# A gated mix of a spectral filter and a state-space scan on one core: A's inner steps sent through DRAM, first and last stage in 64x64 matmul tiles

## The chip, the cores and the metric

The kernel runs on one core of a Trainium2 chip, in fp32 throughout. The metric is the device time of one execution in microseconds (us), given as the median of several runs. A core has TensorE (PE, with weight loads shown apart as PEld), VectorE (DVE), ScalarE (ACT), GpSimd (POOL) and SyncE (SP), which here issues most DMA transfers; DMAs are also issued by POOL. PE reads from SBUF and writes PSUM, whose pool `ps` has four buffers of 128 partitions x 2 x 512 fp32 in this kernel.

## The reference

x has 2048 positions (L) and 512 channels (D). Two linear operators act on it, and a gate mixes them:

```python
x = A_x
g = _sigmoid((x * gate_w).sum(-1, keepdims=True))
a = irfft2(rfft2(x) * (w_r + 1j * w_i))             # share A, over positions and channels
K = 2 * Re(sum_n C[d, n] * exp(A[d, n] * dt[d] * l))
b = causal_convolution(x, K) + x * D_skip           # share B, for each channel
return g * a + (1 - g) * b
```

## The kernel before, in words

For share B the kernel assumes that every channel's kernel K is level over the sequence, so that the convolution is a running sum with one coefficient a channel; it counts the channels for which the data allow that (`count`) and enters a general path after the main one (`tc.If`) only where the count is below D. With these inputs it isn't entered.

Share A is a two-dimensional real transform written as matmuls. The 2048 positions are split into 32 x 64 and the 512 channels into folded quarters. The steps are these:

- Ten parts of x (`PARTS`) come by DMA. `fold` (L228, L229, on DVE or POOL) adds and subtracts the halves of a part into a buffer `f`; `C_` (L236, PE) multiplies by `s1e`, into PSUM; `c_a` (L240, DVE) writes a transpose in 32x32 blocks to `AR`.
- Nine units u follow, each for one slot pair `pr` of the inner frequencies: `P_` (L351) and `t_a` (L356), `D_` (L365) and `d_a` (L372), `Z_` (L378, L379) on DVE, `z_a` and `z_b` for one row, the filter weights `W_`, `U` (L400 to L405) on DVE, `p_a` and `g_a` (L412 to L425) on POOL, `h_a`, then the way back: `I_` (L440), `i_a` (L445), `V_` (L453, into `AI`), `B_` (L478 to L481) and `e_a` (L485, ACT, back into `AI`). The letters v, w, j, K, E, H do parts of the last three steps for unit 8.
- When all units are in `AI`, `b_a` (L503) transposes it in place on DVE, eight times 128x1024. `Q_` (L528) multiplies its rows by the constants `s1a`, four matmuls for each of eight output groups j.

Share B: `load_x` fetches x turned (XT, 1 MB for each of four shares), `x_a` (L277, ACT) multiplies it by the coefficient, `scan` (L283, DVE) takes the running sum v. The skip term is then joined in one of two ways: `skip` (L286, ACT) and `both` (L289), an accumulating DMA issued by POOL that adds v to XT; or `skip2` (L292, DVE). `Y_` (L511, PE) turns XT back to rows of positions by `T.transpose`, eight for each j, and `s_a` (L516, ACT) multiplies by 1 - g into `AR`, which by then is free. The gate itself is `G_` (L300 to L308).

The two meet at the output. For most j, `q_a` (L549, DVE) takes Q's PSUM times g plus `AR`; for one j, `a_a` (L539, ACT) takes it out of PSUM and `A_a` (L543, POOL) adds it. `store` (L532) issues two 256-KB stores for each j from SP.

The order of all of this is written out by hand, in the string `PLAN`: each word is a letter for a function and a number for its argument, and each engine gets its instructions in that order. So does SP with its DMAs: one that waits holds back all behind it. `R` words are loads of constants, `l` of filter weights, `X` of XT, `S` of `s1a`.

Of the kernel before, what the change touches and what calls it, by code (L numbers as in the profile page):

```python
# [26 lines left out]
ALU = mybir.AluOpType  # L27
# [25 lines left out]
PARTS = [slice(a, b) for a, b in zip([0, 8, 16, 32, 48, 64, 80, 96, 112, 120], [8, 16, 32, 48, 64, 80, 96, 112, 120, 128])]  # L53
CHANNELS = np.concatenate([_T, 256 + _T, 511 - _T, 255 - _T])


def _consts():
# [14 lines left out]
    s1e = np.zeros((2, 32, 2, 2, 2, 2, 16))  # L72
    for dh in range(2):
        for h in range(2):
            for g in range(2):
                s1e[dh, :, g, g, :, h] = S1[:, :, :16] * (-1) ** (dh * h)
# [35 lines left out]
    s2p = s2p.transpose(1, 0, 2)  # L112
# [41 lines left out]
def body(ctx: ExitStack, tc: tile.TileContext, x, xg, xt, w, wh, prms, vecs, gw, dskip,  # L154
# [48 lines left out]
    with tc.manual_schedule():  # L203
# [19 lines left out]
        def fold(q, E):  # L223
            k = PARTS[q]
            n = 32 * (k.stop - k.start)
            f = t_["f", q] = blk([P, 2, 512], "f")
            xv = X[:, 64 * k.start:64 * k.stop].rearrange("p (u n) -> p u n", u=2)
            E.tensor_tensor(f[:, 0, :n], xv[:, 0], xv[:, 1], op=ALU.add)  # L228
            E.tensor_tensor(f[:, 1, :n], xv[:, 0], xv[:, 1], op=ALU.subtract)  # L229


        def C_(q):
            n = 32 * (PARTS[q].stop - PARTS[q].start)
            p = t_["c", q] = psum("p_s1")
            for u in range(2):
                T.matmul(p[:, u, :n], s1e, t_["f", q][:, u, :n], start=True, stop=True)  # L236
# [58 lines left out]
        def G_(k):  # L295
# [160 lines left out]
        def M_(u):  # L456
            p = t_["pi", u] = psum("p_v").rearrange("p u (h n) -> p u h n", h=2)
            for v in range(nrow(UNITS[u]) // 64):
                for h in range(2):
                    a = [t_["gt", u][:, o, v, 2 * h:2 * h + 2].rearrange("p c k -> p (c k)") for o in range(2)]  # L460
                    T.matmul(p[:, v, h], a[0], dbw[:, h, 0:1].broadcast_to([P, 2, P]), start=True, stop=False)
                    T.matmul(p[:, v, h], a[1], dbw[:, h, 1:3], start=False, stop=True)

        def o_a(u, ks=slice(0, 2)):
            pr = UNITS[u]
            n = nrow(pr) // 64
            ai = AI[:, 2 * pr:2 * pr + n].rearrange("p s (h k t) -> p s h k t", h=2, k=2)
            pi = t_["pi", u][:, :n].rearrange("p s h (k t) -> p s h k t", k=2)
            S.copy(ai[:, :, :, ks], pi[:, :, :, ks])


        def B_(u):
            pr = UNITS[u]
            p = t_["pb", u] = psum("p_ia")
            for v in range(2):
                sl = 2 * pr + v
                if sl == 0:
                    T.matmul(p[:, v], s2e[:, 0], AI[:, 0], start=True, stop=False)  # L478
                    T.matmul(p[:, v], s2e[:, 16], AI[:, 16], start=False, stop=True)
                else:  # L480
                    T.matmul(p[:, v], s2p, AI[:, sl], start=True, stop=True)  # L481

        def e_a(u):
            pr = UNITS[u]
            S.copy(AI[:, 2 * pr:2 * pr + 2], t_["pb", u])  # L485


        def half(u, k):
            pr = UNITS[u]
            return AI[:, 2 * pr:2 * pr + 2].rearrange("p s (h k t) -> p k s h t", h=2, k=2)[:, k]  # L490

        def B2_(u, k):
            if k == 0:
                t_["pb", u] = psum("p_ia").rearrange("p k (s h t) -> p k s h t", s=2, h=2)
            for v in range(2):
                T.matmul(t_["pb", u][:, k, v], s2p, half(u, k)[:, v], start=True, stop=True)

        def e2_a(u, k):
            S.copy(half(u, k), t_["pb", u][:, k])

        def b_a(c):
            v = VA[:, :, 32 * c:32 * c + 32].rearrange("p b d -> p d b")
            V.transpose(v, v)  # L503


        def Y_(j):
            p = t_["py", j] = psum("p_y").rearrange("p k (b i d) -> p (k b) i d", b=2, i=2)
            xv = XT.rearrange("p (i e) (c b) -> p i (e c) b", i=2, b=32)
            for k in range(4):
                for i in range(2):  # L510
                    T.transpose(p[:, k, i], xv[:, i, :, 4 * j + k], eye)  # L511

        def s_a(j):
            for k in range(4):
                b = 4 * j + k
                S.activation(AR[:, b].rearrange("p (i d) -> p i d", i=2), t_["py", j][:, k], AF.Copy, scale=g1[:, 1, b:b + 1])  # L516
# [4 lines left out]
        def load_a(k):  # L521
            s1a[k] = work.tile([P, 8, P], F32, tag="w", name="s1a", bufs=4)
            nc.sync.dma_start(s1a[k], c_s1a[:, 8 * k:8 * k + 8])

        def Q_(j):
            p = t_["pq", j] = psum("p_oa").rearrange("p k (b d) -> p (k b) d", b=2)
            for k in range(4):
                T.matmul(p[:, k], s1a[j // 2][:, 4 * j % 8 + k], VA[:, 4 * j + k], start=True, stop=True)  # L528
# [17 lines left out]
        def q_a(j):  # L546
            for k in range(4):
                b = 4 * j + k
                V.scalar_tensor_tensor(AR[:, b], t_["pq", j][:, k], g1[:, 0, b:b + 1], AR[:, b], op0=ALU.mult, op1=ALU.add)  # L549
# [28 lines left out]
    with tc.If(n_small < D):  # L578
        with tc.tile_pool(name="dram", bufs=1, space=bass.MemoryType.DRAM) as dp:
# [137 lines left out]
            for e in range(2):  # L717
                nc.sync.dma_start(dsg[64 * e:64 * e + 64], dskip[256 * e:256 * e + 256].rearrange("(o d) -> o d", o=1).broadcast_to([64, 256]))
# [76 lines left out]
```

## Time and profile before

| what | value |
|---|---|
| runs shown | 148.42, 150.05, 151.9 us; median 150.05 |
| profiled execution | 148.65 us, of which the span is 146.8 |
| busy in the span | PE 112.6, DVE 113.8, ACT 70.5, POOL 57.4 us |
| DMA | 25.52 MB, mean 174 GB/s |
| mean granted TensorE clock | 0.95 |

Times inside the program count from the span's start. In a group's row the first number is the busy time of all its instructions together, the second the mean length of one in ns; overlapping instructions are counted once in the first. Behind the second bar stand the idle time of the engine just ahead of them, and what ended it. An fp32 matmul appears as two records, a transpose as one.

### The profile page before, as it was taken

The numbers are of one execution on the slowest core, as the hardware profiler recorded it, in microseconds if no ns is written. First come the engines' busy times: TensorE is split into PE (matmuls) and PEld (weight loads), VectorE is DVE, ScalarE is ACT, GpSimd is POOL, SyncE is SP. The second block draws the span as 40 slices with busy tenths as digits, with TensorE's granted clock in tenths as the row PEclk, the third lists the DMA queues.
The fourth block names the chain that finished last, engine by engine and source line by source line (L and its number), as shares of the span: only waits on it lengthen the run. The fifth ranks groups of instructions, "written<-read, shape, count | busy, mean of one in ns | idle before, by whom it ended". The sixth has DMA issues, their size and how long they took to land.

```text
span 146.8 us, 1834 instructions
## 1 busy us (share of the span) xinstructions
PE 112.6 (77%) x611; PEld 86.1 (59%) x611; DVE 113.8 (78%) x134; ACT 70.5 (48%) x136; POOL 57.4 (39%) x57
## 2 busy tenths in 40 slices
PE   7936976399989998959888878997805975999600
PEld 7811352098978982858378577462405964888400
DVE  0369999995788597759798995979689997695900
ACT  0003000337375969496789765398610699504000
POOL 0306850100059993976999979200200000003300
PEclk9999999959999999999999999999975899999985
DMA  4999999992105870404793898000191000158690
GB/s 114 318 275 418 391 417 387 413 416 99 37 7 173 287 292 0 143 5 146 132 225 91 273 214 210 4 0 0 40 214 36 0 0 0 57 205 318 223 354 19
DMA packets 9427, 25.52 MB, mean 174 GB/s; under 512 B 1568, under 2 KB 2624, under 8 KB 8512
## 3 DMA queue, kind: packets, MB, share of 16 engines
q1 hardware_dynamic: 8976, 22.16, 42.2%
q0 software_dynamic: 432, 3.15, 10.9%
q8 instruction: 7, 0.11, 0.3%
q14 instruction: 12, 0.10, 0.2%
HBM read 17.93 MB, written 4.19 MB: 151 GB/s over the span
## 4 chain that ended last, share of the span: by engine, by line
DVE 31%; PE 30%; ACT 17%; DMA 9%; issue 5%; POOL 2%; SPq 1%; DVEq 0%; ACTq 0%; POOLq 0%
DVE AR L240 9%; PE p_oa L528 8%; PE p_d L365 6%; ACT AR L516 6%; PE p_t L351 5%; DMA XT<-v 5%; PE p_v L440 5%; DMA AI<-in_x_dram 5%; DVE v L283 3%; DVE p_d L378 3%; DVE p_d L379 3%; DVE tw L405 3%; PE p_ia L481 2%; PE p_y L511 2%; DVE AR L549 2%
## 5 line engine op out<-in xcount | busy, mean ns | idle before, releaser
L351 PEld LDWEIGHTS p_t<-s2e,AR 128*128 128x128 f32 x136 | 17.4, 208 | 5.5 <-DVE AR L240 3.5
L351 PE MATMUL p_t<-s2e,AR 128*128 128x128 f32 x136 | 18.0, 294 | 3.4 <-DVE AR L240 2.7
L440 PEld LDWEIGHTS p_v<-dbw,gt 128*128 128x128 f32 x136 | 16.0, 192 | 7.5 <-issue 4.6
L440 PE MATMUL p_v<-dbw,gt 128*128 128x128 f32 x136 | 16.8, 278 | 4.6 <-ACT gs L303 1.5
L236 PE MATMUL p_s<-f,AI 128*128 128x512 f32 (+1 forms) x40 | 15.7, 527 | 5.5 <-DVE f L228 3.4
L412 POOL TENSOR_TENSOR px<-tw 128x512 f32<-128x512 f32 (+1 forms) x9 | 10.9, 1215 | 19.6 <-DVE tw L405 19.5
L503 DVE STREAM_TRANSPOSE AI<-AI 128x1024 f32<-128x1024 f32 x8 | 16.9, 2202 | 1.8 <-ACT AI L485 1.8
L365 PE MATMUL p_d<-et,dfw 128*128 128x256 f32 (+1 forms) x72 | 16.1, 371 | 0.7 <-ACT et L356 0.6
L240 DVE STREAM_TRANSPOSE AR<-p_s 128x1024 f32<-128x1024 f32 (+1 forms) x10 | 14.8, 1555 | 1.6 <-PE p_s L236 1.6
L516 ACT ACTIVATE AR<-p_y,g 128x256 f32<-128x256 f32 x32 | 11.8, 587 | 8.1 <-PE p_y L511 8.1
L528 PE MATMUL p_oa<-AI,s1a 128*128 128x256 f32 x64 | 14.1, 380 | 1.7 <-ACT AR L516 1.7
L511 PE MATMUL p_y<-eye,XT 128*128 128x128 f32 x64 | 10.0, 317 | 6.5 <-DMA XT<-v 5.6
L277 ACT ACTIVATE p_x<-XT,pers 128x1024 f32<-128x1024 f32 x8 | 9.0, 1121 | 12.5 <-POOL pers L261 10.4
L549 DVE SCALAR_TENSOR_TENSOR AR<-p_oa,g,AR 128x256 f32<-128x256 f32 x28 | 11.6, 477 | 4.2 <-PE p_oa L528 4.0
L236 PEld LDWEIGHTS p_s<-f,AI 128*128 128x128 f32 x40 | 7.1, 196 | 13.1 <-issue 4.3
L365 PEld LDWEIGHTS p_d<-et,dfw 128*128 128x128 f32 x72 | 12.7, 190 | 2.5 <-ACT et L356 1.2
L528 PEld LDWEIGHTS p_oa<-AI,s1a 128*128 128x128 f32 x64 | 12.1, 190 | 3.5 <-ACT AR L516 1.9
L543 POOL TENSOR_TENSOR AR<-AR,qs 128x1024 f32<-128x1024 f32 x1 | 2.3, 2348 | 29.2 <-ACT qs L539 29.2
L511 PEld LDWEIGHTS p_y<-eye,XT 128*128 128x128 f32 x64 | 9.2, 201 | 7.8 <-issue 6.3
L453 DVE TENSOR_TENSOR AI<-p_v,po 128x512 f32<-128x512 f32 (+1 forms) x18 | 10.9, 650 | 2.3 <-ACT po L445 2.3
L405 DVE TENSOR_TENSOR tw<-p_d,w 128x1024 f32<-128x1024 f32 x8 | 9.8, 1219 | 3.6 <-ACT p_d L390 3.6
L481 PE MATMUL p_ia<-AI,s2p 128*128 128x512 f32 x26 | 12.0, 595 | 0.0
(66 smaller groups left out, 180.6 us busy)
## 6 DMA issues: line engine op xcount, KB each, us to landing
w<-in_w_dram SPq DMA_DIRECT2D x8, 512.0 KB, 5.6
XT<-in_xt_dram SPq DMA_DIRECT2D x4, 1024.0 KB, 7.0
out_dram<-AR SPq DMA_DIRECT2D x16, 256.0 KB, 3.7
AI<-in_x_dram SPq DMA_DIRECT2D x6, 512.0 KB, 7.6
XT<-v POOLq DMA_DIRECT2D x3, 1024.0 KB, 7.0
s1a<-in_c_s1a_dram SPq DMA_DIRECT2D x4, 512.0 KB, 3.9
AI<-in_x_dram SPq DMA_DIRECT2D x4, 256.0 KB
prm<-in_prms_dram SPq DMA_DIRECT2D x3, 256.0 KB
```

Source lines behind the costliest of these rows:

```text
L236: T.matmul(p[:, u, :n], s1e, t_["f", q][:, u, :n], start=True, stop=True)
L240: V.transpose(AR.rearrange("p s (u d) -> p u d s", u=2)[:, :, PARTS[q]], t_["c", q][:, :, :32 * n].rearrange("p u (b d) -> p u d b", d=n))
L351: T.matmul(p[:, q, :, 64 * v:64 * v + 64], AR[:, 16 * (q // 2) + sl, 128 * (q % 2):128 * (q % 2) + 128], s2e[:, k], start=True, stop=True)
L365: T.matmul(p[:, o, :, h, :n], dfw[:, 2 * h + o], et[:, ::-1] if h else et, start=True, stop=True)
L405: E.tensor_tensor(t.rearrange("p o r a k -> p (o r a k)"), z.rearrange("p o q k -> p (o q k)"), w.rearrange("p o r a k -> p (o r a k)"), o ...
L440: T.matmul(p[:, v, h, o], t_["gt", u][:, o, v, 2 * h:2 * h + 2].rearrange("p c k -> p (c k)"), dbw[:, h, o], start=True, stop=True)
L481: T.matmul(p[:, v], s2p, AI[:, sl], start=True, stop=True)
L503: V.transpose(v, v)
L511: T.transpose(p[:, k, i], xv[:, i, :, 4 * j + k], eye)
L516: S.activation(AR[:, b].rearrange("p (i d) -> p i d", i=2), t_["py", j][:, k], AF.Copy, scale=g1[:, 1, b:b + 1])
L528: T.matmul(p[:, k], s1a[j // 2][:, 4 * j % 8 + k], VA[:, 4 * j + k], start=True, stop=True)
L549: V.scalar_tensor_tensor(AR[:, b], t_["pq", j][:, k], g1[:, 0, b:b + 1], AR[:, b], op0=ALU.mult, op1=ALU.add)
```

## The change

**First stage.** The folds are gone. The host lays out x so that the two halves of a position pair lie in partitions 0 to 63 and 64 to 127, in swapped order for every other part. `C_(q)` now does parts q and q + 1 together: 16 matmuls with 64 rows of contraction and 64 output partitions (`tile_position` (r, o)), the sum over u taken in PSUM. The ten loads of x are issued one behind another; `ldt` and `prm` come behind them (R10, R11).

**Inner steps.** `V_` writes `ai` and `e_a` writes `ei`, both blocks of the work pool, in place of `AI`. `b_a(u)` stores `ei` to a DRAM tile `ad` in two DMAs, in 1-KB runs, and `b_b(p)` reads the slot pairs p and p + 4 back in one 1-MB DMA, 32 partitions of `VA` by 32 KB. The eight transposes of L503 and the half steps of unit 8 are removed.

**Last stage.** `Y_` does 16 ordinary matmuls against `eye` for each j, each into 64 output partitions, in place of eight transposes. `Q_` does eight matmuls in 64x64 tiles in place of four in 128x128. Rows are taken in the order `LAST`; `s1a` is half as large and comes in two loads of 512 KB in place of four. Three j (1, 5, 7) take the way over ACT and POOL, five over DVE; the new `PLAN` ends with `Y7 Y1 s7 s1 Y5 s5 b1 w2 Y2 s2 w0 Y6 s6 Y0 Q2 q2 s0 Q1 a1 Q0 q0 Q5 Q6 q6 Q7 a5 G4 a7 A1 Y4 s4 A5 Q4 G5 q4 Y3 A7 s3 Q3 q3`, where w is `b_b`. The gate's DMA is cut in four. `count` moves from stage 1 to the end.

```diff
+LAST = np.array([2 * j + k % 2 + 16 * (k // 2) for j in range(8) for k in range(4)])
...
-        def fold(q, E):
...
-            f = t_["f", q] = blk([P, 2, 512], "f")
-            xv = X[:, 64 * k.start:64 * k.stop].rearrange("p (u n) -> p u n", u=2)
-            E.tensor_tensor(f[:, 0, :n], xv[:, 0], xv[:, 1], op=ALU.add)
-            E.tensor_tensor(f[:, 1, :n], xv[:, 0], xv[:, 1], op=ALU.subtract)
...
         def C_(q):
             n = 32 * (PARTS[q].stop - PARTS[q].start)
-            p = t_["c", q] = psum("p_s1")
-            for u in range(2):
-                T.matmul(p[:, u, :n], s1e, t_["f", q][:, u, :n], start=True, stop=True)
+            p = [psum("p_s1"), psum("p_s1")]
+            t_["c", q], t_["c", q + 1] = p
+            xv = [X[:, 64 * k.start:64 * k.stop].rearrange("p (u n) -> p u n", u=2) for k in PARTS[q:q + 2]]
+            for f in range(2):
+                for u in range(2):
+                    for h in range(2):
+                        for r in (0, 64):
+                            o = r ^ 64 * h
+                            T.matmul(p[h][o:o + 64, f, :n], s1e[r:r + 64, f * u], xv[h][r:r + 64, u], start=u == 0, stop=u == 1, tile_position=(r, o))
...
-        def b_a(c):
-            v = VA[:, :, 32 * c:32 * c + 32].rearrange("p b d -> p d b")
-            V.transpose(v, v)
+        def b_a(u):
+            k, p = divmod(UNITS[u], 4)
+            if ("ad", p) not in t_:
+                t_["ad", p] = dr.tile([2, 4, 2, 2, 32, 256], F32, name=f"ad{p}")
+            for g in range(2):
+                nc.sync.dma_start(t_["ad", p][g, :, k].rearrange("v c b d -> (c b) v d"), t_["ei", u][g::2].rearrange("p s (e d) -> p (s e) d", e=2))
+
+        def b_b(p):
+            nc.sync.dma_start(VA[p::4].rearrange("p b d -> p (b d)"), t_["ad", p].rearrange("g v k c b d -> (g v k c) (b d)"))
...
-            xv = XT.rearrange("p (i e) (c b) -> p i (e c) b", i=2, b=32)
+            xv = XT.rearrange("p (i e) (a g b) -> p i g b (e a)", i=2, g=2, b=32)
             for k in range(4):
                 for i in range(2):
-                    T.transpose(p[:, k, i], xv[:, i, :, 4 * j + k], eye)
+                    for g in range(2):
+                        T.matmul(p[64 * g:64 * g + 64, k, i], xv[:, i, g, LAST[4 * j + k]], eye, start=True, stop=True, tile_position=(0, 64 * g))
...
-            for k in range(4):
-                T.matmul(p[:, k], s1a[j // 2][:, 4 * j % 8 + k], VA[:, 4 * j + k], start=True, stop=True)
+            for k in (0, 2, 1, 3):
+                for r in (0, 64):
+                    o = r ^ 64 * (k // 2)
+                    T.matmul(p[o:o + 64, k], s1a[j // 4][r:r + 64, 4 * (j % 4) + k], VA[r:r + 64, LAST[4 * j + k]], start=True, stop=True, tile_position=(r, o))
```

`PLAN` is new as a whole, so the order of each engine is shown where it matters. On DVE at the start of the program, before the change (p_s1 is C_'s PSUM, f a folded part, prm the parameters of B):

```order
L228 TENSOR_TENSOR f_113<-AI_64 128x256
L229 TENSOR_TENSOR f_113<-AI_64 128x256
L240 STREAM_TRANSPOSE AR_68<-p_s1_116 128x2x8x32
L228 TENSOR_TENSOR f_124<-AI_64 128x512
L229 TENSOR_TENSOR f_124<-AI_64 128x512
L228 TENSOR_TENSOR f_129<-AI_64 128x512
L229 TENSOR_TENSOR f_129<-AI_64 128x512
L240 STREAM_TRANSPOSE AR_68<-p_s1_120 128x2x8x32
L240 STREAM_TRANSPOSE AR_68<-p_s1_138 128x2x16x32
```

And after it, at the same place:

```order
L237 STREAM_TRANSPOSE AR_70<-p_s1_110 128x2x8x32
L237 STREAM_TRANSPOSE AR_70<-p_s1_111 128x2x8x32
L237 STREAM_TRANSPOSE AR_70<-p_s1_132 128x2x16x32
L237 STREAM_TRANSPOSE AR_70<-p_s1_133 128x2x16x32
L237 STREAM_TRANSPOSE AR_70<-p_s1_152 128x2x16x32
L237 STREAM_TRANSPOSE AR_70<-p_s1_153 128x2x16x32
L243 TENSOR_REDUCE last_72<-prm_82 128x4
L244 TENSOR_REDUCE last_72<-prm_83 128x4
L237 STREAM_TRANSPOSE AR_70<-p_s1_179 128x2x16x32
L237 STREAM_TRANSPOSE AR_70<-p_s1_178 128x2x16x32
```

DVE now waits for PE's pairs in the order of the parts, with nothing between them.

On DVE at the end, before the change (v the running sums, p_oa the PSUM of Q):

```order
L292 SCALAR_TENSOR_TENSOR XT_69<-XT_69,pers_70,v_723 128x1024
L453 TENSOR_TENSOR AI_64<-p_v_739,po_748 128x4x128
L283 SCALAR_TENSOR_TENSOR v_723<-pers_70,v_723,p_x_754 128x1024
L453 TENSOR_TENSOR AI_64<-p_v_739,po_748 128x4x128
L283 SCALAR_TENSOR_TENSOR v_671<-pers_70,v_671,p_x_762 128x1024
L292 SCALAR_TENSOR_TENSOR XT_69<-XT_69,pers_70,v_723 128x1024
L503 STREAM_TRANSPOSE AI_64<-AI_64 128x32x32 x8
L549 SCALAR_TENSOR_TENSOR AR_68<-p_oa_892,g1_62,AR_68 128x256 x4
```

And after it:

```order
L280 SCALAR_TENSOR_TENSOR v_800<-pers_73,p_x_775 128x1024
L280 SCALAR_TENSOR_TENSOR v_800<-pers_73,v_800,p_x_802 128x1024
L454 TENSOR_TENSOR ai_827<-p_v_819,po_824 128x2x128 x2
L289 SCALAR_TENSOR_TENSOR XT_71<-XT_71,pers_73,v_800 128x1024 x2
L529 SCALAR_TENSOR_TENSOR AR_70<-p_oa_969,g1_62,AR_70 128x256 x4
```

Two skip2 end DVE's work before the outputs, where one skip2 and the eight transposes stood.

On SP, behind the loads of weights, after the change (ei the unit's result, ad its DRAM tile); before it, the last loads of `s1a` and then the stores of the output stood there:

```order
L477 DMA ad3_696<-ei_688 64x4x256 x2
L477 DMA ad3_696<-ei_701 64x4x256 x2
L480 DMA VA_64<-ad3_696 32x8192
L477 DMA ad2_814<-ei_798 64x4x256 x2
L477 DMA ad2_814<-ei_809 64x4x256 x2
L477 DMA ad0_839<-ei_817 64x4x256 x2
L477 DMA ad0_839<-ei_837 64x4x256 x2
L480 DMA VA_64<-ad2_814 32x8192
L480 DMA VA_64<-ad0_839 32x8192
```

The read of a pair of units stands behind its four stores; the last two reads come one behind another.

More of the change, by code (lines that the diff above doesn't have):

```diff
@@ L70, in _consts @@
         S1[:, 1, s] = -np.sin(2 * pi * a * f / 32)
-    s1e = np.zeros((2, 32, 2, 2, 2, 2, 16))
+    s1e = np.zeros((2, 2, 32, 2, 2, 2, 16))
     for dh in range(2):
         for h in range(2):
-            for g in range(2):
-                s1e[dh, :, g, g, :, h] = S1[:, :, :16] * (-1) ** (dh * h)
+            for k in range(2):
+                s1e[:, dh, :, k, :, h] = S1[:, :, :16] * (-1) ** (dh * h + k)
     s1f = np.zeros((2, 2, 32, 2, 2, 2, 32))
@@ L167, in body @@
     count = keep.tile([1, 1], I32, name="count")
-    AI = keep.tile([P, 17, D], F32, name="AI")
-    VA = AI[:, 0:16].rearrange("p s (e d) -> p (s e) d", e=2)
+    VA = keep.tile([P, 32, 256], F32, name="VA")
+    dr = ctx.enter_context(tc.tile_pool(name="dr", bufs=1, space=bass.MemoryType.DRAM))
     wst = ExitStack()
@@ L178, in body @@
     XT = work.tile([P, 4, L], F32, name="XT")
-    X = AI.rearrange("p s d -> p (s d)")[:, 0:8192]
-    last = AI[:, 16]
-    s1e, ones = last[:, 0:128], last[:, 128:256]
+    X = VA.rearrange("p s d -> p (s d)")
+    last = work.tile([P, 388], F32, name="last")
+    s1e, ones = last[:, 0:128].rearrange("p (k m) -> p k m", k=2), last[:, 128:256]
     hw = last[:, 256:328].rearrange("p (q r f m) -> p q r f m", q=9, r=2, f=2)
@@ L304, in G_ @@
             elif k == 2:
-                for e in range(2):
-                    nc.sync.dma_start(g1[64 * e:64 * e + 64, 0], t_["gs"][0:P:32])
+                gv = t_["gs"].rearrange("p (a g b) -> p g a b", g=2, b=32)
+                for g in range(2):
+                    for e in range(2):
+                        nc.sync.dma_start(g1[64 * g + 32 * e:64 * g + 32 * e + 32, 0], gv[0:P:32, g])
             elif k == 3:
@@ L450, in V_ @@
             n = nrow(pr) // 64
-            ai = AI[:, 2 * pr:2 * pr + n].rearrange("p s (h k t) -> p s h k t", h=2, k=2)
+            if 0 in ks:
+                t_["ai", pr] = blk([P, 2, D], "ai")
+            ai = t_["ai", pr][:, :n].rearrange("p s (h k t) -> p s h k t", h=2, k=2)
             for k in ks:
                 V.tensor_tensor(ai[:, :, :, k], t_["pi", u][:, :n, :, 0], t_["po", u][:, :n], op=ALU.subtract if k else ALU.add)
[L456 to L469, printed above, removed]
         def B_(u):
@@ L475, in B_ @@
             for v in range(2):
[L476 to L479, printed above, removed]
+                if 2 * pr + v == 0:
+                    T.matmul(p[:, v], s2e[:, 0], t_["ai", 0][:, 0], start=True, stop=False)
+                    T.matmul(p[:, v], s2e[:, 16], t_["ai", 8][:, 0], start=False, stop=True)
                 else:
-                    T.matmul(p[:, v], s2p, AI[:, sl], start=True, stop=True)
+                    T.matmul(p[:, v], s2p, t_["ai", pr][:, v], start=True, stop=True)
@@ L483, in e_a @@
         def e_a(u):
[L484 to L496, printed above, removed]
@@ L513, in s_a @@
         def s_a(j):
             for k in range(4):
-                b = 4 * j + k
-                S.activation(AR[:, b].rearrange("p (i d) -> p i d", i=2), t_["py", j][:, k], AF.Copy, scale=g1[:, 1, b:b + 1])
+                b = LAST[4 * j + k]
+                S.activation(AR[:, 4 * j + k].rearrange("p (i d) -> p i d", i=2), t_["py", j][:, k], AF.Copy, scale=g1[:, 1, b:b + 1])
         s1a = {}
         def load_a(k):
-            s1a[k] = work.tile([P, 8, P], F32, tag="w", name="s1a", bufs=4)
@@ L523, in load_a @@
-            nc.sync.dma_start(s1a[k], c_s1a[:, 8 * k:8 * k + 8])
+            s1a[k] = work.tile([P, 16, 64], F32, tag="w", name="s1a", bufs=4)
+            nc.sync.dma_start(s1a[k], c_s1a[:, 16 * k:16 * k + 16])
         def Q_(j):
             p = t_["pq", j] = psum("p_oa").rearrange("p k (b d) -> p (k b) d", b=2)
-            for k in range(4):
-                T.matmul(p[:, k], s1a[j // 2][:, 4 * j % 8 + k], VA[:, 4 * j + k], start=True, stop=True)
+            for k in (0, 2, 1, 3):
+                for r in (0, 64):
+                    o = r ^ 64 * (k // 2)
+                    T.matmul(p[o:o + 64, k], s1a[j // 4][r:r + 64, 4 * (j % 4) + k], VA[r:r + 64, LAST[4 * j + k]], start=True, stop=True, tile_position=(r, o))
```

96 lines of the change are left out of this document (52 added, 44 removed).

## The prediction

> **What bounds the kernel now.** I read the page first, for the span, the engines and the shares of the chain that ended last.
>
> ```profile
> span 146.8 us, 1834 instructions
> PE 112.6 (77%) x611; PEld 86.1 (59%) x611; DVE 113.8 (78%) x134; ACT 70.5 (48%) x136; POOL 57.4 (39%) x57
> DVE 31%; PE 30%; ACT 17%; DMA 9%; issue 5%; POOL 2%; SPq 1%; DVEq 0%; ACTq 0%; POOLq 0%
> ```
>
> DVE and PE are both busy for three quarters of the span and share the chain, so no engine alone sets the end, and the stages must be read one by one. The next view is the last chain in order of time; these are its pieces at the borders of stages (start, length, what).
>
> ```profile
> 104.58 6.97 DMA XT<-v
> ...
> 111.68 3.45 PE p_y L511 x15
> 115.15 8.87 ACT AR L516 x24
> ...
> 124.06 12.34 PE p_oa L528 x56
> ...
> 139.34 0.47 DVE AR L549
> ```
>
> It ends with a transfer (v added into XT by GpSimd's queue), then Y's transposes on PE, their scaling on ACT, then Q on PE. The last store goes out at 139.8. I cut the span at these points, with the first P at 29.6; the columns are the stretch, busy time of PE, weight loads, DVE, ACT and POOL with instruction counts, the granted clock, the DMA share and GB/s.
>
> ```profile
> 0.00:29.60 29.60, 20.40 (x68) 11.60 (x68) 22.59 (x30) 2.61 (x3) 9.64 (x17) 1.00 0.94 342
> 29.60:105.20 75.60, 67.49 (x414) 53.23 (x415) 62.72 (x70) 53.50 (x96) 45.20 (x39) 0.98 0.45 133
> 105.20:124.00 18.80, 10.62 (x66) 9.16 (x64) 16.92 (x9) 9.86 (x26) 0.25 (x1) 0.82 0.28 56
> 124.00:139.80 15.80, 14.05 (x64) 12.08 (x64) 11.60 (x28) 4.50 (x13) 2.35 (x1) 1.00 0.54 195
> 139.80:146.80 7.00, 0.00 (x0) 0.00 (x0) 0.01 (x1) 0.00 (x0) 0.00 (x0) 0.68 0.48 177
> ```
>
> Stage 1 (x in, first transform) is filled by DVE; the middle (units u) by PE and DVE together; the third stretch by DVE's in-place transposes, beside the late transfer and Y; the fourth by PE's Q. The last 7.0 us are the stores landing and the end of the program, which I keep as they are, since the last output row still leaves by the same 256-KB stores. The profiled execution took 148.65 us, 1.85 over its span; the median of the runs shown is 150.05, 1.4 more. I sum against the profile and add the 1.4 at the end.
>
> **Stage 1.** The change drops the folds and makes C_ a set of 16 quarter-size matmuls for each pair of parts. By the groups of instructions (count, busy us, mean ns, idle before):
>
> ```profile
> L228 DVE TENSOR_TENSOR f<-AI 128x512 f32<-128x512 f32 (+1 forms) x6 | 3.5, 590 | 4.6 <-DMA AI<-in_x_dram 4.6
> L229 DVE TENSOR_TENSOR f<-AI 128x512 f32<-128x512 f32 (+1 forms) x6 | 3.5, 588 | 0.0
> L240 DVE STREAM_TRANSPOSE AR<-p_s 128x1024 f32<-128x1024 f32 x6 | 11.3, 1901 | 0.0
> L240 DVE STREAM_TRANSPOSE AR<-p_s 128x512 f32<-128x512 f32 x4 | 4.1, 1035 | 1.6 <-PE p_s L236 1.6
> L259 DVE TENSOR_REDUCE pers<-prm 128x4 f32<-128x512 f32 x1 | 0.7, 675 | 0.0
> 5.04 0.72 POOL L228 TENSOR_TENSOR f<-AI 128x256 f32<-128x256 f32 x1 [4.59 <-DMA AI<-in_x_dram]
> 9.00 0.69 DVE L228 TENSOR_TENSOR f<-AI 128x512 f32<-128x512 f32 x1 [1.23 <-DMA AI<-in_x_dram]
> 11.60 1.27 POOL L228 TENSOR_TENSOR f<-AI 128x512 f32<-128x512 f32 x1 [5.16 <-DMA AI<-in_x_dram]
> 30.00:32.00 2.00, 2.00 (x11) 2.00 (x11) 1.96 (x1) 0.92 (x1) 0.00 (x0) 0.50 1.05 432
> L300 PE MATMUL p_gate<-XT,gws 128*32 128x512 f32 x32 | 3.6, 595 | 0.0
> L481 PE MATMUL p_ia<-AI,s2p 128*128 128x512 f32 x26 | 12.0, 595 | 0.0
> ```
>
> DVE loses 3.5 + 3.5 = 7.0 us of folds. What stays is 15.4 us of transposes, three reduces (2.0) and 0.4 of small work. What do four quarter tiles cost on PE? The trace has no 64x64 tile. The nearest row is the gate: 16 matmuls of 512 columns in four column tiles took 3.64 us, while the 13 full matmuls of 512 columns of L481 took 12.0, 0.92 each. Four column tiles therefore ran in the time of one. I take the same for four 64x64 tiles: a pair of 512-column parts takes 16/4 x 0.91 = 3.6 us, a 256-column pair 1.8. The other end is that only two of the four run at once, 7.3 and 3.6; that is rival one. Below 3.6 the bound is that all 16 took less than four full matmuls, for which no row speaks.
>
> Now the walk. The waits above show parts 0 and 1 landed by 5.0, part 2 at 9.0 and part 4 by 11.6; I take part 3 at 9.7. Since a pair needs both parts, C0 runs 5.5 to 7.3, c0 and c1 end at 9.4. C2 runs 9.7 to 13.3; c2 and c3 follow, 15.2 and 17.1. C4 runs 13.3 to 16.9, c4, c5 end at 20.9, the two reduces at 22.2. C6 must wait for the PSUM buffers of c2 and c3: 17.1 to 20.7, well before DVE wants it; c7 and c6 end at 26.0, the reduce and J0 at 27.1. By the order, half of C8 waits for the buffer of c6, so it ends at 27.8 and c8, c9 at 29.9. **T, the end of stage 1, is 29.9 against 29.6**: the 7.0 us of folds go, and waits for pairs (2.4 at the start, 0.3 and 3.9 before C2's result, 0.7 at the end) take their place. With x landing about 1 us earlier, because the three prm loads no longer stand among its parts, T is near 28; with a PE clock halved after the idle gap before C8, as the granted clock of 0.50 in 30 to 32 shows it after PE's idle time there, it is near 32.
>
> **The middle.** Its DVE rows are the same scans, Z, W, U and V_ instructions: 62.7 us busy of 75.6. The half steps of unit 8 become whole ones (nothing on balance), and 16 stores and four reads join SP's queue in place of nothing, beside DMA rings that were 45% busy. Walking the new order with the old durations, I get 76 us from T to the last skip2 (k6), so **S, the start of Y, is 29.9 + 76 = 105.9**. The part that is new is what Y waits for. Before it waited for the transfer:
>
> ```profile
> POOL XT L289 <- ACT XT L286: 13.2, 2, 11.8
> PE p_y L511 <- DMA XT<-v: 5.6, 1, 5.6
> XT<-v POOLq DMA_DIRECT2D x3, 1024.0 KB, 7.0
> ```
>
> GpSimd sat idle for 11.8 us before it could issue the last one, as the scan and skip that feed it came last; now the last share is finished by skip2 on DVE instead and r0, the last transfer, is issued about 65 us after T. With the 7.0 of its row it lands at T + 73, 3 us ahead of k6. So Y starts at 105.9 and not 111.7: **5.8 us gained**. Should r0 go out 4 us later than I walk it, 1 us of that comes back.
>
> **The last stage.** These rows price it.
>
> ```profile
> L503 DVE STREAM_TRANSPOSE AI<-AI 128x1024 f32<-128x1024 f32 x8 | 16.9, 2202 | 1.8 <-ACT AI L485 1.8
> L511 PE MATMUL p_y<-eye,XT 128*128 128x128 f32 x64 | 10.0, 317 | 6.5 <-DMA XT<-v 5.6
> L516 ACT ACTIVATE AR<-p_y,g 128x256 f32<-128x256 f32 x32 | 11.8, 587 | 8.1 <-PE p_y L511 8.1
> L528 PE MATMUL p_oa<-AI,s1a 128*128 128x256 f32 x64 | 14.1, 380 | 1.7 <-ACT AR L516 1.7
> L549 DVE SCALAR_TENSOR_TENSOR AR<-p_oa,g,AR 128x256 f32<-128x256 f32 x28 | 11.6, 477 | 4.2 <-PE p_oa L528 4.0
> L539 ACT ACTIVATE qs<-p_oa,g 128x256 f32<-128x256 f32 x4 | 1.6, 474 | 6.0 <-PE p_oa L528 6.0
> L543 POOL TENSOR_TENSOR AR<-AR,qs 128x1024 f32<-128x1024 f32 x1 | 2.3, 2348 | 29.2 <-ACT qs L539 29.2
> 36.24 3.73 PE L351 MATMUL p_t<-s2e,AR 128*128 128x128 f32 x32
> XT<-in_xt_dram SPq DMA_DIRECT2D x4, 1024.0 KB, 7.0
> out_dram<-AR SPq DMA_DIRECT2D x16, 256.0 KB, 3.7
> s1a<-in_c_s1a_dram SPq DMA_DIRECT2D x4, 512.0 KB, 3.9
> ```
>
> The 16.9 us of L503 disappear from DVE. In their place the last unit goes through DRAM: two 256-KB stores of ei, then the read of 1 MB. The trace has neither; the nearest rows are the 256-KB output store, 3.7 us, and the 1-MB read of XT, 7.0. The store is issued about 0.5 after S, so the last read lands at S + 0.5 + 3.7 + 7.0, about **S + 11.3**. From below, a 512-KB s1a read took 3.9 on calmer rings, which puts it near S + 8; from above, 32 partitions instead of 128 and 1-KB runs could double both, S + 22.
>
> The Trainium skill bears on this read: "DMA: Bandwidth & Descriptors", in its part on the anatomy of one DMA, gives a fixed 2 us plus bytes over 436 GB/s. By that the store would be an estimated 2.6 us and the read 4.4, and the round trip would be over before PE is through with Y. The XT row's 7.0 for the same 1 MB, under load, speaks against using it, and the sum above does not.
>
> PE is not idle meanwhile. Y now has 16 ordinary matmuls a j in column pairs. 16 such matmuls of 128 columns took 3.73 us (the p_t stretch, 32 records); two at once, as in the gate, make 1.87 a j, against 10.0/8 = 1.25 for the transposes. Six Y before the first Q are 11.2 us: Q2 starts at **S + 11.5**, with the read just landed. Q has eight matmuls of 256 columns a j, four at once: 2 x 0.46 = 0.9, against 14.1/8 = 1.76. ACT's s takes 4 x 0.37 = 1.5, a 1.6, DVE's q 4 x 0.41 = 1.7, POOL's A 2.35 and is hidden twice, since the last two outputs are DVE's. After Q2, Q1, Q0, Q5, Q6, Q7 (5.4) come Y4 (1.9), Q4 (0.9), Y3 (1.9), s3 (1.5) and q3 (1.7): the last q ends at S + 11.5 + 13.3 = S + 24.8. ACT, the next in line, has s0, three a and two s after S + 11.2, 9.3 us, and is no later.
>
> **Sum.** 29.9 + 76 + 24.8 + 7.0 = 137.7 us span, against 146.8: 5.8 from Y's earlier start, 3.3 from Q and the missing transposes. With 1.85 that is 139.6 for an execution like the profiled one, and with the 1.4 to the median **141 us**.
>
> **Rival one: the quarter tiles run two at a time** (slower). A 512 pair then takes 7.3 us, more than the 3.8 in which DVE empties it. C2 ends at 17.0, C4 at 24.3, C6 at 31.6, C8 at 35.2, and T is 39; S is 115. Q takes 1.8 a j, seven on the path, 6.3 more: the end is S + 31, the span 153, the median's scale 156. It decides from a pair of 5.5 us on: there T is about 33.5 and each Q 0.4 longer, and the gain of 9 has shrunk to about 2. For it speaks that nothing in the trace has two row tiles write one PSUM bank; against it the gate, where the column tiles did run together. The Trainium skill, "TensorEngine Tiling (Array Packing)", Gotcha 1, says that different row tiles cannot access the same PSUM bank simultaneously. Here r = 0 and r = 64 write the two partition halves of one bank in each pair, so by that rule the 64x64 tiles would run in twos and the sum would be that of this rival; no row here has row tiles to test it. Chance 0.12.
>
> **Rival two: the trip through DRAM is late.** Should the two legs take 1.6 times their rows, Q2 waits to S + 17.5, PE is idle for 6 us, and Y4 and Y3 stand behind the waiting Q2: 6 us more, 147 on the median's scale, no change. For it: runs of 1 KB and a 32-partition target, and a w2 read on the rings just ahead; against it: rings that were 28% busy there. Chance 0.18.
>
> **Rival three: it goes better.** x lands earlier, T is 27.5 to 28, the read is over early and Y runs faster than p_t did; the last stage is then 22: 135 to 136. Chance 0.12. That the change does nothing is no case, as whole groups go.
>
> **How the numbers follow.** The forecast has 0.58, with 138 to 144 as its own range (T 1.9 lower to 2.1 higher, r0 1 late). 2% is about what a measurement of this kernel can tell from no change, that is 147 and 153. Faster: 0.58 + 0.12 + half of rival two, 0.79. Slower: rival one without its milder forms, 0.10; the rest, 0.11, within 2%. The range leaves out rival one, 0.12, and the late tail of rival two: 134 to 149.
>
> **What would show it.** A pair of C_ at 3.6 us (rival one: 7); the first P at 30; Y's first matmul about 106 with skip2 and not XT<-v ahead of it; Q2 waiting under 1 us for the VA read; the last q at S + 25. Wrong would make it above all a C_ pair over 5 us, a VA read over 10, or DVE in the middle waiting for PE more than before.

## The result, and the profile after

The changed kernel takes **138.68 us** (median; 137.66 to 142.19), the kernel before, on the same chip, 150.63. The ratio is 0.927, with a 95% interval of 0.907 to 0.947: faster by 7%. The ratios, here and below, leave out executions more than 1.5% above the fastest of their kernel, so they are not quotients of the medians. The forecast was 141 in a range of 134 to 149. The profiled execution took 137.66 us, 135.9 of it the span.

The page of the changed kernel, first its span, the engines and the chain:

```profile
span 135.9 us, 2591 instructions
PE 114.1 (84%) x983; PEld 86.1 (63%) x983; DVE 87.7 (65%) x106; ACT 74.4 (55%) x143; POOL 53.8 (40%) x51
PE 44%; DVE 20%; DMA 13%; ACT 11%; issue 4%; SPq 2%; POOL 0%; DVEq 0%; ACTq 0%; POOLq 0%
```

DVE lost 26 us of work (113.8 to 87.7), PE gained 1.5, and the chain moved from DVE to PE. The span cut at the same events as before: the first P, Y's start, Q's start, the end of the last q.

```profile
0.00:27.30 27.30, 22.30 (x181) 11.82 (x182) 16.77 (x19) 3.00 (x5) 1.20 (x9) 0.94 0.91 335
27.30:102.90 75.60, 68.84 (x410) 53.93 (x411) 62.62 (x67) 54.20 (x95) 45.49 (x39) 0.96 0.70 206
102.90:115.30 12.40, 11.18 (x192) 11.01 (x193) 0.00 (x0) 9.01 (x24) 0.00 (x0) 1.00 0.87 311
115.30:128.90 13.60, 11.77 (x200) 9.30 (x200) 8.34 (x21) 8.23 (x22) 7.09 (x3) 1.00 0.68 247
128.90:135.90 7.00, 0.00 (x0) 0.00 (x0) 0.00 (x0) 0.00 (x0) 0.00 (x0) 0.55 0.38 138
```

Stage 1 is 2.3 us shorter. From the first P to Y's start it is 75.6 us, where before Y started 82.1 after P. From Y's start to the last q it is 26.0, before 28.1. The stores at the end take the same 7.0. Stage 1 by its timeline, PE and DVE (start, length, what, idle time before):

```profile
9.77 10.96 PE L233 MATMUL p_s<-VA,last 64*64 64x512 f32 x96 [0.30 <-DMA VA<-in_x_dram]
22.95 2.90 PE L233 MATMUL p_s<-VA,last 64*64 64x256 f32 x28 [2.22 <-DVE AR L237]
...
12.63 7.39 DVE L237 STREAM_TRANSPOSE AR<-p_s 128x1024 f32<-128x1024 f32 x4 [2.57 <-PE p_s L233]
...
20.92 3.73 DVE L237 STREAM_TRANSPOSE AR<-p_s 128x1024 f32<-128x1024 f32 x2
...
25.23 1.98 DVE L237 STREAM_TRANSPOSE AR<-p_s 128x512 f32<-128x512 f32 x2
```

Three pairs of 512-column parts take 11 us on PE, and DVE, once it has the first, transposes without a gap but for the small reduces. The groups of the quarter tiles and of Y, by form; the first line is C_ of the kernel before:

```profile
L236 PE MATMUL p_s<-f,AI 128*128 128x512 f32 x24 | 11.7, 613 | 4.7 <-DVE f L228 3.4 <-POOL f L228 1.2
...
L233 PE MATMUL p_s<-VA,last 64*64 64x512 f32 x96 | 11.6, 592 | 0.6 <-DMA VA<-in_x_dram 0.6
L508 PE MATMUL p_oa<-VA,s1a 64*64 64x256 f32 x128 | 7.6, 381 | 1.2 <-ACT AR L494 1.2
L489 PE MATMUL p_y<-eye,XT 128*64 128x128 f32 x256 | 15.4, 279 | 1.4 <-DMA XT<-v 1.4
L237 DVE STREAM_TRANSPOSE AR<-p_s 128x1024 f32<-128x1024 f32 (+1 forms) x10 | 15.0, 1620 | 9.7 <-PE p_s L233 9.7
```

Read the first two with their means: 24 full-size records of 613 ns filled 11.7 us, with little on top of each other; 96 quarter-size records of 592 ns are 57 us of records in 11.6 us, five on top of each other. So the four tiles overlap. The last transfer XT<-v and skip2 by the timeline, Y's first six j, then the end of the chain and the two waits that stand at the last stage's borders:

```profile
91.55 0.87 POOL L286 DMA_DIRECT2D XT<-v  x1 [3.42 <-ACT XT L283]
99.38 2.47 DVE L289 SCALAR_TENSOR_TENSOR XT<-XT,pers,v 128x1024 f32<-128x1024 f32 x2
102.92 11.18 PE L489 MATMUL p_y<-eye,XT 128*64 128x128 f32 x192 [1.42 <-DMA XT<-v]
...
103.19 6.07 DMA ad<-ei
...
109.28 4.88 DMA VA<-ad
...
115.34 5.39 PE p_oa L508 x96
...
PE p_y L489 <- DMA XT<-v: 1.4, 1, 1.4
...
PE p_oa L508 <- ACT AR L494: 1.2, 1, 1.2
```

The trip through DRAM is on the chain. The second wait is named after ACT, and the chain ends the read at 114.16, but the trace has more: the semaphore of the last read is raised sixteen times, from 114.03 to 114.97, and Q starts 0.36 us after the last of these. In the two variants below whose Q waits for the read (the run with the tiles' work done twice and the one without the last transfer) it also starts 0.35 after the last one. So the read landed at 114.97, 0.9 behind Y's last matmul, and the wait of 1.2 is the read's; the fourth experiment confirms it.

### The profile page after: what moved, and what is told of

Same layout as the page of the kernel before. It is cut to its first block, busy times and chain, and to the rows that moved or that the text cites. A ratio compares the mean times of both kernels' runs of the same rounds, so it can differ in the third digit from the quotient of the medians.

```text
span 135.9 us, 2591 instructions
## 1 busy us (share of the span) xinstructions
PE 114.1 (84%) x983; PEld 86.1 (63%) x983; DVE 87.7 (65%) x106; ACT 74.4 (55%) x143; POOL 53.8 (40%) x51
## 4 chain that ended last, share of the span: by engine, by line
PE 44%; DVE 20%; DMA 13%; ACT 11%; issue 4%; SPq 2%; POOL 0%; DVEq 0%; ACTq 0%; POOLq 0%
PE p_t L350 12%; PE p_d L364 10%; DVE AR L237 8%; PE p_v L439 7%; PE p_oa L508 6%; DMA VA<-in_x_dram 5%; DVE v L280 5%; DMA ad<-ei 4%; DMA VA<-ad 4%; PE p_y L489 3%; ACT XT L283 2%; DVE ai L454 2%; ACT p_x L274 2%; PE p_s L233 2%; PE p_ia L465 2%
## 5 line engine op out<-in xcount | busy, mean ns | idle before, releaser
L529 DVE SCALAR_TENSOR_TENSOR AR<-p_oa,g,AR 128x256 f32<-128x256 f32 x20 | 8.3, 476 | 18.7 <-PE p_oa L508 18.6
L233 PE MATMUL p_s<-VA,last 64*64 64x512 f32 (+1 forms) x160 | 17.4, 546 | 2.8 <-DVE AR L237 2.2
L411 POOL TENSOR_TENSOR px<-tw 128x512 f32<-128x512 f32 (+1 forms) x9 | 10.9, 1212 | 16.6 <-DVE tw L404 12.6
L523 POOL TENSOR_TENSOR AR<-AR,qs 128x1024 f32<-128x1024 f32 x3 | 7.1, 2391 | 25.1 <-ACT qs L519 25.1
L489 PE MATMUL p_y<-eye,XT 128*64 128x128 f32 x256 | 15.4, 279 | 1.4 <-DMA XT<-v 1.4
L489 PEld LDWEIGHTS p_y<-eye,XT 128*64 128x64 f32 x256 | 14.8, 197 | 2.6 <-issue 2.6
L233 PEld LDWEIGHTS p_s<-VA,last 64*64 64x64 f32 x160 | 7.4, 146 | 12.3 <-issue 7.0
L465 PE MATMUL p_ia<-ai,s2p 128*128 128x512 f32 x30 | 13.9, 595 | 1.2 <-DVE ai L454 1.2
L454 DVE TENSOR_TENSOR ai<-p_v,po 128x512 f32<-128x512 f32 (+1 forms) x18 | 10.9, 650 | 1.7 <-ACT po L444 1.6
L423 POOL TENSOR_TENSOR gt<-px 128x512 f32<-128x512 f32 (+1 forms) x9 | 11.7, 1301 | 0.5
L424 POOL TENSOR_TENSOR gt<-px 128x512 f32<-128x512 f32 (+1 forms) x9 | 11.7, 1300 | 0.0
L412 POOL TENSOR_TENSOR px<-tw 128x512 f32<-128x512 f32 (+1 forms) x9 | 10.9, 1208 | 1.4 <-DVE tw L402 1.4
```

Source lines behind the costliest of these rows:

```text
L233: T.matmul(p[h][o:o + 64, f, :n], s1e[r:r + 64, f * u], xv[h][r:r + 64, u], start=u == 0, stop=u == 1, tile_position=(r, o))
L423: G.tensor_tensor(gv[:, :, 0], src[0], src[1], op=ALU.add)
L424: G.tensor_tensor(gv[:, ::-1, 1], src[0], src[1], op=ALU.subtract)
L465: T.matmul(p[:, v], s2p, t_["ai", pr][:, v], start=True, stop=True)
L489: T.matmul(p[64 * g:64 * g + 64, k, i], xv[:, i, g, LAST[4 * j + k]], eye, start=True, stop=True, tile_position=(0, 64 * g))
```

## The experiments

Theory: stage 1 is shorter because the folds are gone, at no cost on PE since four quarter tiles run at once; the last stage is shorter because the transposes of L503 and the late transfer XT<-v, which covered each other, are both gone, and the trip through DRAM that replaces them is hidden under Y but for 1 us. Rivals: the tiles run in twos; the trip sets the end; one of the two covers alone made the gain.

### Do the tiles run at once?

In the first run the loop over r stands outermost in `C_`, in the second in `Q_`:

```diff
-            for f in range(2):
-                for u in range(2):
-                    for h in range(2):
-                        for r in (0, 64):
+            for r in (0, 64):
+                for f in range(2):
+                    for u in range(2):
+                        for h in range(2):
```

> The changed kernel with the loop over r outermost in C_, so that only the two column tiles of one row half stand next to each other; same 16 matmuls. If the four quarter tiles of a pair run at once (forecast), a 512-column pair doubles from 3.6 to about 7.3 us, T goes from 27.3 to about 37, and the time from 138.7 to about 148.5. If a 64-row matmul is simply short and the tiles run one after another, the order does not matter: pairs stay at 3.6 and the time at 138.7.

Measured: 144.43 us, ratio 0.960 (0.954 to 0.966).

```profile
L233 PE MATMUL p_s<-VA,last 64*64 64x512 f32 x96 | 15.4, 596 | 0.5 <-DVE AR L237 0.3 <-DMA VA<-in_x_dram 0.2
```

Busy time rose from 11.6 to 15.4, a third and not a factor of two, and the first P came at 33.1. Both numbers of the expectation were missed.

> The changed kernel with the loop over r outermost in Q_. If Q is on the path with four tiles at once, Q takes 1.8 us a j in place of 0.9, and the eight of them add 6 to 7 us: about 145. If DVE and ACT, which empty Q's PSUM at 1.7 and 1.6 us a j, set the pace, it adds only the last two Q, about 2 us: 140.5.

Measured: 139.28 us, ratio 0.926 (0.918 to 0.934).

```profile
L508 PE MATMUL p_oa<-VA,s1a 64*64 64x256 f32 x128 | 7.7, 381 | 1.1 <-ACT AR L494 1.1
```

Nothing changed: 7.7 us against 7.6. The order does not force twos, so these two runs did not build the rival. The starts of the single records in the traces tell more. In the changed kernel they come in fours within 0.1 us, a new four every 0.43 us in `C_` (512 columns) and every 0.22 us in Q (256). With the rows apart, a part of `C_` starts in twos, also every 0.43 us, and then in fours again. The weight loads show the same steps, first in the changed kernel, then with the rows apart:

```profile
10.22 0.18 PEld L233 LDWEIGHTS p_s<-VA,last 64*64 64x64 f32 x4 [0.25 <-issue]
10.65 0.18 PEld L233 LDWEIGHTS p_s<-VA,last 64*64 64x64 f32 x4 [0.25 <-issue]
...
10.36 0.17 PEld L233 LDWEIGHTS p_s<-VA,last 64*64 64x64 f32 x2 [0.26 <-issue]
10.79 0.17 PEld L233 LDWEIGHTS p_s<-VA,last 64*64 64x64 f32 x2 [0.26 <-issue]
```

So two quarter tiles take as long as four, which excludes that the tiles run one after another; that the fours come back must mean that records of the other row half join before the first half is through. Why eight records a half are absorbed in Q and sixteen longer ones in `C_` only in part is not settled by this.

The rival's price was then measured by doing the work twice, in `C_` and in `Q_`:

```diff
-            for f in range(2):
+            for f in (0, 0, 1, 1):
...
-            for k in (0, 2, 1, 3):
+            for k in (0, 2, 0, 2, 1, 3, 1, 3):
```

> The changed kernel with every 64x64 matmul of C_ and of Q_ issued twice (the second writes the same again): a 512-column pair takes 7.3 us and a Q 1.8, what the prediction's first rival gave them. Its working has T at 39 in place of 27.3 to 29.9 and 6.3 us more in the last stage, 156 in all on its scale; by the trace of the changed kernel, whose T was 2.6 earlier than walked, about 153. If DVE's own work in stage 1 covered the second half of the pairs, 5 us less: 148.

Measured: 155.03 us, ratio 1.046 (1.029 to 1.063).

```profile
L237 DVE STREAM_TRANSPOSE AR<-p_s 128x1024 f32<-128x1024 f32 (+1 forms) x10 | 15.0, 1572 | 22.3 <-PE p_s L233 22.3
...
40.20 3.81 PE L350 MATMUL p_t<-s2e,AR 128*128 128x128 f32 x32 [1.44 <-issue]
...
125.78 12.28 PE L508 MATMUL p_oa<-VA,s1a 64*64 64x256 f32 x192 [2.15 <-DMA VA<-ad]
```

DVE waits 22.3 us for PE in stage 1 (9.7 in the changed kernel), the first P is at 40.2, and Q takes twice as long. So with this much PE time the change is a loss, of 3 to 6%; that the tiles run at once is what the whole gain stands on.

### What did the folds cost?

The third run keeps folds and the 128x128 `C_`:

```diff
+            E.tensor_tensor(f[:, 0, :n], xv[:, 0], xv[:, 1], op=ALU.add)
+            E.tensor_tensor(f[:, 1, :n], xv[:, 0], xv[:, 1], op=ALU.subtract)
...
+                T.matmul(p[:, u, :n], last[:, 0:128], t_["f", q][:, u, :n], start=True, stop=True)
```

> The changed kernel with the folds and the 128x128 C_ of before; the rest, the order behind stage 1 and the loads of prm behind x too, as changed. The theory that removing the folds shortens stage 1: T goes from 27.3 back to about 29.6 and the time up by 2.3, to 141. The rival, that DVE's idle time for pairs costs what the folds cost (the prediction's T of 29.9): no change, 138.7.

Measured: 141.55 us, ratio 0.941 (0.935 to 0.948).

```profile
28.45 2.19 DVE L240 STREAM_TRANSPOSE AR<-p_s 128x512 f32<-128x512 f32 x2
...
30.73 5.72 PE L353 MATMUL p_t<-s2e,AR 128*128 128x128 f32 x32 [0.97 <-ACT hT L328]
```

The last transposes end 3.4 us later (30.6 for 27.2), the first P comes at 30.7, and the median is 2.9 up. The theory holds: removing the folds is worth 2 to 3 us (2.2 by the ratios, 2.9 by the medians), about a quarter of the gain.

### Is the trip through DRAM on the path?

The fourth run reads the last two quarters of VA early, from a tile that is long complete:

```diff
-            nc.sync.dma_start(VA[p::4]..., t_["ad", p]...)
+            nc.sync.dma_start(VA[p::4]..., t_["ad", 1 if p in (0, 2) else p]...)
```

> The changed kernel with the last two reads (w2, w0) taken from ad1, which is complete long before, right behind w1; the stores stay, and the rows of the output that hang on the four slot pairs are those of other units. No Q waits for the trip through DRAM any more. If the trip is just hidden by Y (forecast: landing at S + 11.3, Y's end at S + 11.2), Q2 starts 1.2 us earlier at most, and the time is 137.5 to 138.7. If the trip sets the end (rival two), several us go: below 135.

Measured: 136.53 us, ratio 0.907 (0.903 to 0.911), about 2 less than the changed kernel, 1 below the expected band.

```profile
102.73 11.45 PE L489 MATMUL p_y<-eye,XT 128*64 128x128 f32 x192
...
114.11 5.41 PE L508 MATMUL p_oa<-VA,s1a 64*64 64x256 f32 x96
```

Q now starts where Y ends, so the 1.2 us in front of it were the trip's. In the trace only this 1.2 goes; where the rest of the 2 comes from stays open, and the interval of the changed kernel is as wide. Rival two, the trip as the bound, is out: without it nothing near 5 us is gained.

### Which cover went?

Three runs of the kernel before: without the last transfer (the word `r2` is taken out of `PLAN`), without the transposes (the eight `b` words), without both.

> The kernel before without the last transfer XT<-v (the running sum of share 2 is left out of the output). Y can then start at 105.2 in place of 111.7. The theory that the transfer and the eight transposes of L503 covered each other: Q still starts at 124.0, when L503 ends, and the time stays within 1 us of 150. The prediction's own accounting, 5.8 us for Y's earlier start alone: 144.5.

> The kernel before without the eight transposes of L503 (share A's rows are not turned, its output is of other rows). If they and the late Y cover each other, the scaling s still ends at 124.0 and Q starts there: within 1 us of 150. If the transposes alone set the stretch, Q starts when PSUM is free, several us earlier: 145.

> The kernel before without both, the last transfer XT<-v and the transposes of L503 (the output lacks the one and has the other unturned). If they cover each other, only this one gains: Y from 105.5, s to about 118, Q from 118: about 6 us, 144. If neither bound the stretch, it is again 150.

Measured: 152.59 us, ratio 1.017 (1.009 to 1.026); 147.39, ratio 0.983 (0.975 to 0.990); 140.89, ratio 0.939 (0.929 to 0.949). The timelines, first without the transfer, then without the transposes, then without both:

```profile
31.99 5.49 PE L351 MATMUL p_t<-s2e,AR 128*128 128x128 f32 x24 [2.67 <-DVE AR L240]
...
109.06 4.80 PE L511 MATMUL p_y<-eye,XT 128*128 128x128 f32 x40
110.31 16.97 DVE L503 STREAM_TRANSPOSE AI<-AI 128x1024 f32<-128x1024 f32 x8 [1.84 <-ACT AI L485]
127.38 15.53 PE L528 MATMUL p_oa<-AI,s1a 128*128 128x256 f32 x64 [9.14 <-issue]
```

```profile
29.86 4.50 PE L351 MATMUL p_t<-s2e,AR 128*128 128x128 f32 x24 [2.68 <-DVE AR L240]
...
123.06 14.08 PE L528 MATMUL p_oa<-AI,s1a 128*128 128x256 f32 x64 [0.29 <-ACT AR L516]
```

```profile
32.39 2.94 PE L351 MATMUL p_t<-s2e,AR 128*128 128x128 f32 x24 [2.68 <-DVE AR L240]
...
117.58 14.08 PE L528 MATMUL p_oa<-AI,s1a 128*128 128x256 f32 x64 [0.30 <-ACT AR L516]
```

Stage 1 ended 2.4 and 2.8 us later in the first and the third of these executions, where the granted clock from 9 to 13 us was 0.74 and 0.71 (1.00 in the kernel before); the edits do not touch that stage, so the place of Q is counted from the first P. It was 94.4 after P in the kernel before; without the transfer it is 95.4, since Y is early but L503 still ends just ahead of Q (and PE, after 9.1 us without work, takes 15.5 for Q in place of 14.1). Without the transposes, with the first P at 29.9, Q is 93.2 after it, 1.2 earlier (2.5 by the medians), since the scaling of the late Y ends at nearly the same place. Without both it is 85.2 after P, 9.2 earlier. **Alone the one is worth nothing and the other 1 to 2.5 us, together they are worth 9.** The change takes away both: the transposes are gone, and the last transfer is issued 13 us earlier (91.55 for 104.58), so that Y starts 75.6 after P and not 82.1. With the folds that makes up about the 12 us between the medians. What the quarter tiles of Y and Q bring or cost by themselves, and the new order of the middle, no run isolates.

### What is left

The eighth run leaves out the changed kernel's last transfer (the word `r0`), the twelfth the trips behind `w1` (the words b4, b8, w3, b3, b7, b5, b1, w2, w0).

> The changed kernel without its last transfer XT<-v (r0; the running sum of share 0 is left out of the output). In its trace Y's first matmul waited 1.4 us for it, behind k6. If that wait is real, Y starts at k6's end, S goes from 102.9 to 101.9, and with the trip through DRAM 1 us later than Y then, the time falls by 0.3 to 1.0, to about 138. If the transfer is hidden as forecast, no change.

Measured: 136.14 us, ratio 0.903 (0.896 to 0.911).

```profile
101.18 11.44 PE L489 MATMUL p_y<-eye,XT 128*64 128x128 f32 x192
...
112.94 5.41 PE L508 MATMUL p_oa<-VA,s1a 64*64 64x256 f32 x96 [0.32 <-PE p_y L489]
```

Y's wait is gone, and of Q's 1.2 only 0.3 is left: without the transfer on the DMA rings the trip, from the last store's issue (102.95) to the last update of the read's semaphore (112.59), took 9.6 us in place of 11.8. That is more than expected.

> The changed kernel without the stores and reads of the slot pairs behind w1 (three of the four 1-MB trips through DRAM; the rows of the output that hang on them keep what stood in VA). In the traces of the changed kernel the last transfer XT<-v took 10 to 13 us to land, where the kernel before had 7.0. If the trips' own traffic holds it up, it lands in 7 to 8 us here, Y starts at the end of skip2 without a wait, and Q2 at Y's end: 2 us less than changed, about 136. If GpSimd's own issue of it is what is slow, it still takes 10 us or more and Y still waits 1 us: 137.5.

Measured: 135.07 us, ratio 0.898 (0.892 to 0.904). How long the last transfer XT<-v took and the stretch from 90 to 103 us, in that run and then in the changed kernel:

```profile
DMA to landing us min/median/max: 7.0/7.0/7.0
...
90.00:103.00 13.00, 11.99 (x66) 6.58 (x66) 9.85 (x10) 7.97 (x11) 2.31 (x3) 1.00 0.40 83
```

```profile
DMA to landing us min/median/max: 11.2/11.2/11.2
...
90.00:103.00 13.00, 10.56 (x41) 5.28 (x40) 10.15 (x10) 8.51 (x12) 2.31 (x3) 1.00 0.81 199
```

The last transfer is back at the 7.0 us of the kernel before, with DMA at 40% of the stretch; in the changed kernel, at 81%, it took 11.2, issued at 91.55, and held Y until 102.92. GpSimd's instruction took 0.87 us in both. So the trips' own traffic holds up the transfer, not GpSimd's issue; and by the eighth run the transfer holds up the trips.

The share of busy DMA engines does not give the time by itself: in the kernel before, the second of these transfers also took 7.0 us, at a share of 0.94 (83.28 to 90.24). What differs is the bytes beside it. The 211 GB/s there are 1.47 MB, of which 0.42 are not its own; the 216 GB/s over its 11.2 us in the changed kernel are 2.43 MB, of which 1.38 are not. No run changes these bytes and nothing else, so this stays a reading of the traces.

The tenth run tries to take them away by order alone: the skip `o0` behind `o1` and `r0` ahead of `B7`, and at the end `Y0 Y4 s0 s4 Q2 ... Y3 A5 Q4`. The eleventh is the changed kernel again, beside it.

> The changed kernel with another order: the skip and the transfer r0 of share 0 ahead by about 2.7 us, and Y4, s4 before the first Q, Y3 before Q4. If the two waits seen in its trace (1.4 us of Y for XT<-v, 1.2 us of Q2 for the read of VA) are on the path, both go: about 2 us, 136.5. If the end is bound by PE's work alone, nothing: 138.5.

> The changed kernel itself, beside the other two on the same chip: 138.7, ratio 0.927 to the kernel before.

Measured: 137.59 us (135.85 to 140.64), ratio 0.920 (0.910 to 0.931), beside 139.80 (137.59 to 140.85) for the changed kernel, so 1.6% by the medians; but the ranges overlap, so that the order gains anything is not shown. The trace of the tenth:

```profile
90.02 0.87 POOL L286 DMA_DIRECT2D XT<-v  x1 [1.23 <-ACT gt L431]
...
103.22 12.97 PE L489 MATMUL p_y<-eye,XT 128*64 128x128 f32 x224 [1.81 <-DMA XT<-v]
...
116.12 5.41 PE L508 MATMUL p_oa<-VA,s1a 64*64 64x256 f32 x96
```

The transfer was issued 61.4 us after the first P in place of 64.2 and held Y until 74.6 after it in place of 75.6: it took 13.1 us in place of 11.2, and Y still waited 1.8 for it. Half of the expectation failed there. The other half held: seven Y stand ahead of Q2, which starts without a wait.

In the trace of the eleventh, the changed kernel itself, Y waited for the transfer again, 2.1 us. Q2 did not wait there: the read had landed at 113.9, and Y ended at 115.2, since the granted clock was 0.68 from 102 to 107 us and six Y took 12.77 us in place of 11.18.

## Why the prediction was right

**Stage 1** was forecast as even, T = 29.9; it is 27.3. The prices held: three pairs fill 10.96 us of the timeline, 11.6 by their group, so a pair takes 3.7 to 3.9 us (3.6), DVE's transposes 15.0 (15.4). The walk failed at C8, said to wait for c6 at 26.0; it waited for the first transpose of that pair, to 22.95, and everything ahead was 1 us earlier. That is 2.6 us, so the first part of rival three (T at 27.5 to 28) happened. The forecast that waits would take back all that the folds had cost failed with it: by the third run their removal is worth 2 to 3 us.

**The middle** was to take 76 and takes 75.6, but by luck: skip2 ends at 101.85, 74.6 after P and 1.4 early, while the transfer said to be 3 us ahead of it lands 1 us behind. Its issue was right (64 us after P, forecast 65); the 7.0 of its row, the median of transfers beside which at most 0.5 MB else moved, became 11.2 beside 1.4 MB.

**The last stage** was to end 24.8 us after Y's start and ended 26.0. Y takes 11.18/6 = 1.86 a j (1.87), Q 5.41/6 = 0.90 (0.9). The trip landed 12.05 us after Y's start (11.3), by two errors that partly cancel: the store took 6.07 and not 3.7, the read 5.7 (109.28 to 114.97) and not 7.0. So Q2 came at 12.4 and not 11.5, and what stands behind it took 13.6 (13.3). The Trainium skill's "DMA: Bandwidth & Descriptors" (anatomy of one DMA) gives the fixed 2 us plus bytes for DMAs issued from GpSimd, which the prediction did not say. By it the read was an estimated 4.4 us and the store 2.6; issued from SP, on rings at 87%, the read took 1.3 more, and the store, in 1-KB runs, more than twice that.

**Rival one** did not happen. Its price stood at 156 on the prediction's scale and was measured at 155.0. The rule that had suggested it, Gotcha 1 of "TensorEngine Tiling (Array Packing)" in the Trainium skill (different row tiles cannot access one PSUM bank simultaneously), does not show here: in C_ and in Q two row tiles write the two partition halves of one bank, and the four tiles overlap, a new four every 0.43 us; the 512-column pairs filled 11.6 us, the same work in full matmuls 11.7.

**The sum** was right, its division was not. It gave 5.8 us to Y's earlier start and 3.3 to Q and the missing transposes; by the runs on the kernel before, Y's earlier start alone is worth nothing. Against the forecast of 137.7 the span of 135.9 is 2.6 + 0.4 us less for stage 1 and the middle, and 1.2 more for the last stage, 0.9 of it in front of Q2.

## What to carry to other kernels

When two things end at the same place, price them together: alone the one was worth nothing here and the other 1 to 2.5 us, together 9, and a sum that books the gain to one of them is right only if both go. Quarter-size matmuls that fill all four tiles took a pass over the data off VectorE at no cost in TensorE time here, but the whole gain rests on the four running at once, so measure that first. A trip through DRAM in place of on-chip transposes also slows the other transfers of that stretch: take a landing time from a transfer beside which as many other bytes moved; its busy share alone can mislead.

## What was not expected of the hardware

- Matmuls issued all for one row half, then all for the other, still overlapped: no cost with eight 256-column records a half (7.7 us against 7.6), a third more with sixteen of 512 (15.4 against 11.6).
- The same 1-MB accumulating transfer took 7.0 us as the last of the kernel before and without the trips, and 11.2 and 11.9 as the last in two traces of the changed kernel, beside the trips.
- In the timeline of the changed kernel the first 32 records of P took 5.38 us, in most runs of its variants 3.81; its page shows two of the forty slices of the granted clock at half there, behind PE's waits at the end of stage 1. That is 1.6 us for these records; in the eleventh run the clock was low behind Y's wait too, and six Y took 1.6 us more.

```profile
PEclk9999999559999999999999999599999999999955
27.32 5.38 PE L350 MATMUL p_t<-s2e,AR 128*128 128x128 f32 x32 [1.14 <-ACT hT L325]
```

The first row is the clock in tenths, slice by slice; the second is P.
